# Linear attention and an MLP on one core: chunk-wise attention in eight units, another route for two heads' x, four sums on another engine, and an order made anew

## The chip, the core and the metric

The kernel runs on 1 core of one Trainium2 chip. The metric is device microseconds of one launch, less is better. The engines are named TensorE (PE; its weight loads are PEld), VectorE (DVE), ScalarE (ACT), GpSimd (POOL) and SyncE (SP, whose queue issues the DMAs).

## The reference, cut to what matters

```python
mag = np.sqrt(a_re * a_re + a_im * a_im)
scale = np.minimum(mag, 0.999) / (mag + 1e-06)
a_re_n, a_im_n = (a_re * scale, a_im * scale)
for t in range(S):                       # B, H, S, D = 4, 8, 768, 48
    ar, ai = (a_re_n[:, :, t, :, None], a_im_n[:, :, t, :, None])
    new_re = ar * S_re - ai * S_im
    new_im = ar * S_im + ai * S_re
    kv = np.einsum('bhd,bhe->bhde', k[:, :, t], v[:, :, t])
    S_re, S_im = (new_re + kv, new_im)
    y[:, :, t] = np.einsum('bhd,bhde->bhe', q[:, :, t], S_re)
x = y.transpose(0, 2, 1, 3).reshape(B * S, H * D)        # 3072 x 384
h = x @ w_in                                             # 384 x 2048
out = (0.5 * h * (1.0 + erf(h / sqrt(2)))) @ w_out       # 2048 x 384
```

Inputs are float32 for the attention; the two weights come as 64-bit words that the kernel cuts into a high and a low part.

## The kernel before, in words

**Lanes.** The recurrence is cut in time into four groups (`GROUPS`), each of two chunks: group 0 has chunks of 64 steps, group 1 too, groups 2 and 3 have chunks of 128. Within a chunk the running products of a are scanned from its middle outwards, in 128 lanes, by VectorE (`scan`: two operations a step, tiles `tt` and `bt`), and k and q are scaled by them. A group is done in slices of 8 steps, numbered s = 0 to 23 over all groups (0 to 3 are group 0, 4 to 7 group 1). Each slice needs two sums of squares, of a (`squares_a`, on tile `tab`) and of b (`squares_b`, on tile `a`), which go through ln and exp on ScalarE. `sum_of` makes such a sum on VectorE or GpSimd, or as two matmuls with the identity on TensorE (out to a bank `att`) for the first slices: a's slices 1 to `NGA` - 1 and b's 0 to `NGB` - 1. A tick of slice s handles a's slice s + 2 and b's slice s - 1; b's last slice of a group has the last of its ticks to itself. `against` writes the scaled keys and queries to DRAM (`kq<-xt`).

**Weights.** 32 pieces of the two weight matrices are loaded (`raw`), cut into high and low parts by ScalarE and VectorE (`wh`, `wi_hi`, `wo_lo`, ...), with four TensorE instructions of 384 columns a piece (`po<-wh,ident_r` twice, and one for each part with `minus`).

**Units.** 24 units are 128 tokens each of one batch entry: units 0 to 3 are steps 0 to 127 of the four entries, units 4 to 7 steps 128 to 255, and so on; so units 0 to 7 hold two chunks of 64 and units 8 to 23 one chunk of 128. A unit loads its keys and queries from DRAM (`kqn<-kq`; from unit `UT` = 8 on in pieces for VectorE's transpose), turns them (`kT`, `qT`), makes scores of 128 x 128 for four heads at a time (`att<-qT,kp`, 2 instructions a head), masks them (`kp<-att,causal`, 512 columns), and makes y: from scores and v (`att<-kp,vn`, 2 instructions a head) and from the state of the chunk's start (`att<-qT,st`). In a unit with two chunks the mask also leaves out the scores between the chunks, whose part comes through the state. Then the state is brought forward (`turn_by_pe` or `turn_state`, then `products`). y stands with heads 0 to 5 in places of 48 partitions and heads 6 and 7 apart; ScalarE and VectorE copy it out as a high and a low part, heads 0 to 5 straight to `xT`, heads 6 and 7 to `x67`, from where six copies of 16 KB put it into the free partitions of `xT`. ScalarE's copies also sum each part into a column of `flags`, from which the end of the kernel tells whether the inputs lay in its range.

**Banks.** Of PSUM's eight banks three (`own`, shown as `att`) serve sums, transposes, scores, y and states in turn (`ps_att`), two (`ph`) and three (`po`) serve the MLP. Units 0 and 1 (`early`) take banks for y and states from `ph` and two of `po`. `held` keeps a unit's later banks from falling on the one that holds its y.

**Blocks.** The MLP runs in nine blocks of 2 or 3 units. For each of 16 slices of the hidden layer nine matmuls go to `ph`, ScalarE makes gelu twice (`gh`, `gf`), VectorE or GpSimd the difference (`gl`), and nine (or six) matmuls go to `po`. A block needs the x of all its units before its first matmul.

**The order.** Nothing is issued as it is written down. Each call becomes a step of `Plan`, with its engine (or the engines between which it may choose) and a cost from a table; `order` runs a list scheduler forward and backward over all steps, with ranks that begin from the remaining path plus an offset by kind (`MORE`; `WL` weighs the lanes' VectorE chain, `BIAS` the choice among engines), keeps the best of five passes, and `issue` emits the instructions in that order on each engine. SP's queue issues the DMAs in that order too, each waiting for its input. Since all are emitted by one helper, nearly every row carries the line L427, and rows are told apart by their tiles.

Of the kernel before, what the change touches and what calls it, by code (L numbers as in the profile page):

```python
# [10 lines left out]
F32 = mybir.dt.float32  # L11
# [5 lines left out]
ALU = mybir.AluOpType  # L17
# [3 lines left out]
B, H, S, D = 4, 8, 768, 48  # L21
D2 = 2 * D
BH = B * H
C = 128
NC = S // C
NU = NC * B


GROUPS = ((0, 64), (128, 64), (256, 128), (512, 128))
# [7 lines left out]
NCC = DM // 128  # L37
# [12 lines left out]

flag_n = NSL
flag_x = flag_n + NG
flag_w = flag_x + 2 * NU
NFLAG = flag_w + 2 * NW


def dap(t, offset, dims):
    return bass.AP(t.tensor, t.offset + offset, dims)


def vap(t, dims):
    t = t[:] if not isinstance(t, bass.AP) else t
    return bass.AP(t.tensor, t.offset, [list(t.ap[0])] + dims)
# [23 lines left out]
FIRST_TABLE = TABLES[AF.Ln]  # L87
NEAR = 0.076
LOCK = True
NGA, NGB = 4, 3  # L90
UPE = 6
UT = 8
EARLIER, N_RAW, N_KP = 1, 4, 2
PASSES = 4
N_A = 4
WL = 3.892

MORE = dict(lanes0=141.86, lanes1=-1524.48, lanes2=-2225.65, lanes3=-2095.07, weights=-255.99, units=275.2, blocks=232.24)
BIAS = dict(vector=1.08, scalar=-0.75, gpsimd=1.15, sync=4.42)


class Step:
# [335 lines left out]
def lanes_and_chunks(ctx, tc, flags, a_lanes, x_lanes, v_units, w_in, w_out, out):  # L438
    nc = tc.nc
    pool = lambda name, bufs, **kw: ctx.enter_context(tc.tile_pool(name=name, bufs=bufs, **kw))  # L440
    cst = pool("cst", 1)
    dram = pool("dram", 1, space=DRAM)
    ps = pool("ps", 1, space=PSUM)
    P = Plan(nc, loose=[flags])

    def ring(name, shape, n, dtype=F32, pool=cst):
        return itertools.cycle([pool.tile(shape, dtype, name=f"{name}{i}", tag=f"{name}{i}")[:] for i in range(n)])
# [24 lines left out]
    nc.gpsimd.memset(causal, 1.0)  # L472
    nc.gpsimd.affine_select(causal, causal, pattern=[[1, 128]], compare_op=ALU.is_ge, fill=0.0, base=0, channel_multiplier=-1)

    masks = {C: causal}
    for size in (64,):
        masks[size] = cst.tile([128, 128], F32, name=f"causal{size}")
        nc.gpsimd.tensor_copy(masks[size], causal)
        for t in range(0, C - size, size):
            nc.gpsimd.memset(masks[size][t:t + size, t + size:C], 0.0)  # L480

    wi_hi = cst.tile([128, NFT, NCC, 128], F32R, name="wi_hi")
    wi_lo = cst.tile([128, NFT, NCC, 128], F32R, name="wi_lo")
# [271 lines left out]
    kps = ring("kp", [128, 4, 128], N_KP)  # L755
    xTs = ring("xT", [128, BLK, NCC, 2, 128], 2, F32R)
    x67s = ring("x67", [128, 2, 128], 1, F32R)

    def gains(g):
        p = next(ps_att)  # L760
# [25 lines left out]
    def unit(u):  # L786
# [48 lines left out]
        def bank():  # L835

            p = next(ps_early if early else ps_att)
            return bank() if any(p is x for x in held) else p
# [56 lines left out]
            else:  # L895
                P.vector.tensor_tensor(out=sf, in0=p, in1=sf, op=ALU.add)

        qT, kT, kp, pm = [], [], [], []

        def turn(hh):  # L900
            if by_dve:
# [20 lines left out]
        def scores(hh):  # L922
            p = next(ps_att)
            with P.together():
                for j in range(4):
                    P.tensor.matmul(out=p[:, j * 128:(j + 1) * 128], lhsT=kT[hh][:, j, :], rhs=qT[hh][:, j, :], start=True, stop=True)
            t = kp[hh]
            P.vector.tensor_tensor(out=t, in0=p.rearrange("p (j l) -> p j l", j=4), in1=vap(masks[chunks[0][4]], [[0, 4], [1, 128]]), op=ALU.mult)
            pm.append(t)

        def y(hh):
            with P.together():
                for h in range(hh * 4, hh * 4 + 4):
                    P.tensor.matmul(out=py[h % 2 * 64:h % 2 * 64 + 64, h // 2], lhsT=vn[:, h], rhs=pm[hh][:, h % 4], start=h < 2,
                                    stop=h > 5 and not with_state)
# [8 lines left out]
        if early:  # L947
            turned = {}
            for c0, c1 in zip(chunks[::2], chunks[1::2]):
                add_state(c0, None)  # L950
                turned[c1] = turn_by_pe(c1[0], c1[5])
            held.append(bank())
            py = held[0].rearrange("p (c l) -> p c l", c=4)
            for hh in range(2):
                turn(hh)
                scores(hh)
                y(hh)
                for c in with_state:
                    y_state(c, hh)
            for c in with_state:  # L960
                add_state(c, turned[c])
        else:
            for hh in range(2):
                turn(hh)
                scores(hh)
            held.append(bank())
            py = held[0].rearrange("p (c l) -> p c l", c=4)
            for c in chunks:
                turned = p = None
                if c[0]:  # L970
                    turned = (turn_by_pe if u < UPE else turn_state)(c[0], c[5])
                with P.together():
                    if c is chunks[0]:
                        y(0)
                        y(1)
                    if c[0]:
                        y_state(c, 0)
                        y_state(c, 1)
                    if c[0] < NP - 1:
                        p = products(c, turned)  # L980
                if p is not None:
                    add_state(c, turned, p)
# [2 lines left out]
            xblk[j] = next(xTs)  # L985
        xt, x67 = xblk[j][:, u - first_unit[j]], next(x67s)
        fc = flag_x + 2 * u
        parts = ((py[:, 3], x67[:, 0], x67[:, 1], fc), (py[:, 0:3], xt[:, :, 0], xt[:, :, 1], fc + 1))
        for at, hi, _, f in parts:
            P.scalar.activation(hi, at, AF.Copy, accum_out=flags[:, f:f + 1])  # L990
        for at, hi, lo, _ in parts:
            P.vector.tensor_tensor(out=lo, in0=at, in1=hi.bitcast(F32), op=ALU.subtract)

        for c in range(NCC):
            for p0 in (0, 64):
                P.sync.dma_start(out=xt[p0 + D:p0 + 64, c].bitcast(F32), in_=x67[p0 + c * 16:p0 + c * 16 + 16].bitcast(F32))


    ghs, gls = ring("gh", [128, BLK * C], EARLIER + 1, F32R), ring("gl", [128, BLK * C], EARLIER + 1, F32R)
# [313 lines left out]
```

## Time and profile before

| | us |
|---|---|
| median of 3 runs | 677.06 (673.62 to 678.73) |
| profiled execution, its own time | 673.5 |
| its span, first to last instruction | 671.6 |
| TensorE busy | 617.7 (92%) |
| VectorE busy | 486.4 (72%) |
| ScalarE busy | 442.6 (66%) |
| GpSimd busy | 55.1 (8%) |
| mean granted TensorE clock | 0.964 of full speed |

The profiled execution's own time goes beside the span; the 1.9 us between them lie around it. A share of the whole span is a mean over stages: lanes and weights alone at first, then units and blocks together with the rest of the lanes, then blocks with the last units. The granted clock has two levels, 0.5 (1.2 GHz) and 1.0 (2.4 GHz); a mean between them is a stretch that has both.

### The profile page before, as it was taken

To read this page: it belongs to the slowest core of one execution; us is meant where nothing else is said; L and a number is where in the kernel's file an instruction comes from. 1 tells how busy PE (TensorE), PEld (TensorE's weight loads), DVE (VectorE), ACT (ScalarE), POOL (GpSimd) and SP (SyncE) were. 2 spreads that over 40 slices of the span, in tenths; PEclk is the share of its full clock that TensorE was granted. 3 is DMA by queue.
4 is the path that set the end of the run, shared out by engine and by line. 5 is a ranking of instruction groups with operands and counts; after the bars stand their busy time and mean duration, and the time that the engine had idled before them with its cause. 6 is when DMAs were issued, how large, how long until landed. Compare 5 with 4: busy or idle time off the path is not lost.

```text
span 671.6 us, 13581 instructions
## 1 busy us (share of the span) xinstructions
PE 617.7 (92%) x4882; PEld 568.5 (85%) x4882; DVE 486.4 (72%) x1171; ACT 442.6 (66%) x1104; POOL 55.1 (8%) x95
## 2 busy tenths in 40 slices
PE   4455799988999999999999999999999999999995
PEld 2222477878789989999999998999999999999995
DVE  6999889999999999989959999945552431332121
ACT  8977789998889888787476888653343432233332
POOL 1002103012001100211000001210100000000000
PEclk9877599999999999999999999999999999999998
DMA  9268935758277565788597988697762413010000
GB/s 315 95 150 226 321 120 180 216 154 221 64 207 183 136 138 134 192 146 153 108 153 189 175 223 181 166 157 138 154 121 42 76 57 51 1 47 2 24 1 26
DMA packets 209160, 91.38 MB, mean 136 GB/s; under 512 B 168512, under 2 KB 201408, under 8 KB 209088
## 3 DMA queue, kind: packets, MB, share of 16 engines
q1 hardware_dynamic: 209088, 90.47, 56.6%
q8 instruction: 39, 0.64, 0.4%
q14 instruction: 33, 0.27, 0.1%
HBM read 61.54 MB, written 23.59 MB: 127 GB/s over the span
## 4 chain that ended last, share of the span: by engine, by line
PE 51%; DMA 2%; DVE 2%; ACT 1%; issue 1%; DVEq 0%; SPq 0%
PE po L427 21%; PE ph L427 20%; PE att L427 10%; DMA xt<-in_x_lanes_dram 1%; DMA a<-in_a_lanes_dram 0%; ACT gh L427 0%; DVE tt L427 0%; ACT st L427 0%; DVE bt L427 0%; ACT tab L427 0%; ACT L427 0%; DVE kp L427 0%; DVE gl L427 0%; ACT gf L427 0%; DVE xt L427 0%
## 5 line engine op out<-in xcount | busy, mean ns | idle before, releaser
L427 PE MATMUL ph<-xT,wi_hi 128*128 128x384 f32 (+1 forms) x864 | 208.1, 323 | 1.0 <-ACT gf L427 1.0
L427 PEld LDWEIGHTS ph<-xT,wi_hi 128*128 128x128 f32 x864 | 153.8, 188 | 3.4 <-ACT gf L427 1.8
L427 ACT ACTIVATE gh<-ph 128x384 fp32r<-128x384 f32 (+1 forms) x144 | 65.4, 454 | 135.6 <-PE ph L427 134.8
L427 DVE TENSOR_TENSOR gl<-gf,gh 128x384 fp32r<-128x384 f32 (+1 forms) x133 | 68.7, 517 | 116.0 <-ACT gf L427 115.6
L427 PE MATMUL ph<-xT,wi_lo 128*128 128x384 f32 (+1 forms) x432 | 137.0, 317 | 0.0
L427 PE MATMUL po<-wo_hi,gh 128*128 128x384 f32 x384 | 133.2, 347 | 2.3 <-ACT gh L427 2.2
L427 PE MATMUL po<-wo_lo,gh 128*128 128x384 f32 x384 | 129.6, 338 | 0.0
L427 PE MATMUL po<-wo_hi,gl 128*128 128x384 f32 x384 | 92.4, 342 | 0.0
L427 PEld LDWEIGHTS ph<-xT,wi_lo 128*128 128x128 f32 x432 | 81.2, 188 | 0.0
L427 PEld LDWEIGHTS po<-wo_hi,gh 128*128 128x128 f32 x384 | 72.1, 188 | 5.5 <-ACT gh L427 4.1
L427 PEld LDWEIGHTS po<-wo_lo,gh 128*128 128x128 f32 x384 | 72.3, 188 | 0.4
L427 DVE TENSOR_TENSOR tt<-bt,a 128x192 f32<-128x192 f32 x192 | 69.2, 360 | 0.8
L427 ACT ACTIVATE gf<-ph 128x384 f32<-128x384 f32 (+1 forms) x144 | 65.1, 452 | 2.8 <-DVE gl L427 2.7
L427 PEld LDWEIGHTS po<-wo_hi,gl 128*128 128x128 f32 x384 | 66.0, 188 | 0.9 <-issue 0.2
L427 PE MATMUL po<-wh,ident_r 128*128 128x384 f32 x64 | 34.7, 631 | 24.8 <-ACT wi_lo L427 13.5
L427 PE MATMUL att<-qT,kp 96*128 96x128 f32 x384 | 49.8, 277 | 1.3 <-DVE kp L427 0.9
L427 DVE TENSOR_TENSOR bt<-tt 128x96 f32<-128x96 f32 x192 | 49.1, 256 | 0.8
L427 PEld LDWEIGHTS att<-qT,kp 96*128 96x128 f32 x384 | 47.0, 191 | 2.4 <-ACT a L427 1.7
L427 DVE TENSOR_TENSOR kp<-att,causal 128x512 f32<-128x512 f32 x48 | 32.9, 685 | 19.0 <-PE att L427 18.9
L427 PEld LDWEIGHTS po<-wh,ident_r 128*128 128x128 f32 x64 | 12.5, 230 | 32.1 <-ACT wi_lo L427 16.4
L427 POOL TENSOR_TENSOR gl<-gf,gh 128x384 fp32r<-128x384 f32 (+1 forms) x11 | 12.7, 1158 | 265.6 <-ACT gf L427 207.4
L427 ACT ACTIVATE st<-st,gg 96x48 f32<-96x48 f32 x120 | 28.6, 326 | 1.8 <-DMA m<-st 1.8
(166 smaller groups left out, 1011.6 us busy)
## 6 DMA issues: line engine op xcount, KB each, us to landing
kqn<-kq SPq DMA_DIRECT2D x96, 128.0 KB, 3.8
xt<-in_x_lanes_dram SPq DMA_DIRECT2D x24, 384.0 KB, 4.2
kq<-xt SPq DMA_DIRECT2D x48, 192.0 KB, 3.6
a<-in_a_lanes_dram SPq DMA_DIRECT2D x20, 384.0 KB, 3.5
raw<-in_w_pieces_dram SPq DMA_DIRECT2D x16, 384.0 KB, 4.7
raw<-in_moe_w_out_dram SPq DMA_DIRECT2D x16, 384.0 KB, 5.0
vn<-in_v_units_dram SPq DMA_DIRECT2D x24, 256.0 KB, 3.8
kqn<-kq SPq DMA_DIRECT2D x8, 768.0 KB, 5.8
```

The costliest lines, as they stand in the source:

```text
L427: getattr(getattr(self.nc, engine), name)(*args, **kw)
```

## The change

- Units 0 to 7: scores are made for each chunk of 64 by itself, for all eight heads into one bank, and masked in one VectorE pass of 512 columns; y is made for each chunk into a bank of its own (`y_of`), with the state's part following at once. x is copied out chunk by chunk, so there are four ScalarE and four VectorE parts where there were two of each, with columns of their own in `flags`.
- Units 8 to 23 (`UB` = 8): `x67` goes to a tile in DRAM in one copy of 128 KB, and from there to `xT` in two copies, in place of six copies within SBUF.
- `NGA` goes from 4 to 6 and `NGB` from 3 to 5: the sums of a's slices 4 and 5 and of b's slices 3 and 4 are made by TensorE.
- `WL`, `MORE` and `BIAS` have other values, so that the order of all steps is another one.

```diff
@@ -50,7 +50,7 @@
 flag_n = NSL
 flag_x = flag_n + NG
-flag_w = flag_x + 2 * NU
+flag_w = flag_x + 2 * NU + 2 * sum(size < C for _, size in GROUPS) * B
 NFLAG = flag_w + 2 * NW
@@ -87,16 +87,17 @@
 FIRST_TABLE = TABLES[AF.Ln]
 NEAR = 0.076
 LOCK = True
-NGA, NGB = 4, 3
+NGA, NGB = 6, 5
 UPE = 6
 UT = 8
+UB = 8
 EARLIER, N_RAW, N_KP = 1, 4, 2
 PASSES = 4
 N_A = 4
-WL = 3.892
-MORE = dict(lanes0=141.86, lanes1=-1524.48, lanes2=-2225.65, lanes3=-2095.07, weights=-255.99, units=275.2, blocks=232.24)
-BIAS = dict(vector=1.08, scalar=-0.75, gpsimd=1.15, sync=4.42)
+WL = 5.36
+MORE = dict(lanes0=1180.6, lanes1=-1574.6, lanes2=-4035.5, lanes3=-2920.3, weights=-1612.5, units=-107.0, blocks=-136.5)
+BIAS = dict(vector=0.0, scalar=-1.4, gpsimd=0.7, sync=-4.7)
 class Step:
@@ -472,12 +473,9 @@
     nc.gpsimd.memset(causal, 1.0)
     nc.gpsimd.affine_select(causal, causal, pattern=[[1, 128]], compare_op=ALU.is_ge, fill=0.0, base=0, channel_multiplier=-1)
-    masks = {C: causal}
-    for size in (64,):
-        masks[size] = cst.tile([128, 128], F32, name=f"causal{size}")
-        nc.gpsimd.tensor_copy(masks[size], causal)
-        for t in range(0, C - size, size):
-            nc.gpsimd.memset(masks[size][t:t + size, t + size:C], 0.0)
+    causal64 = cst.tile([128, C // 2], F32, name="causal64")
+    for p0 in (0, 64):
+        nc.gpsimd.tensor_copy(causal64[p0:p0 + 64], causal[p0:p0 + 64, p0:p0 + 64])
     wi_hi = cst.tile([128, NFT, NCC, 128], F32R, name="wi_hi")
     wi_lo = cst.tile([128, NFT, NCC, 128], F32R, name="wi_lo")
@@ -755,6 +753,7 @@
     kps = ring("kp", [128, 4, 128], N_KP)
     xTs = ring("xT", [128, BLK, NCC, 2, 128], 2, F32R)
     x67s = ring("x67", [128, 2, 128], 1, F32R)
+    x67d = itertools.cycle([dram.tile([128, 2, 128], F32, name=f"x67d{i}") for i in range(2)])
     def gains(g):
         p = next(ps_att)
@@ -895,7 +894,7 @@
             else:
                 P.vector.tensor_tensor(out=sf, in0=p, in1=sf, op=ALU.add)
-        qT, kT, kp, pm = [], [], [], []
+        qT, kT, kp, pm, pys = [], [], [], [], []
         def turn(hh):
             if by_dve:
@@ -925,11 +924,37 @@
                 for j in range(4):
                     P.tensor.matmul(out=p[:, j * 128:(j + 1) * 128], lhsT=kT[hh][:, j, :], rhs=qT[hh][:, j, :], start=True, stop=True)
             t = kp[hh]
-            P.vector.tensor_tensor(out=t, in0=p.rearrange("p (j l) -> p j l", j=4), in1=vap(masks[chunks[0][4]], [[0, 4], [1, 128]]), op=ALU.mult)
+            P.vector.tensor_tensor(out=t, in0=p.rearrange("p (j l) -> p j l", j=4), in1=vap(causal, [[0, 4], [1, 128]]), op=ALU.mult)
             pm.append(t)
+        def scores_by_chunk():
+            p = next(ps_att).rearrange("p (h l) -> p h l", h=H)
+            t = kp[0].rearrange("p j l -> p (j l)").rearrange("p (h l) -> p h l", h=H)
+            with P.together():
+                for h in range(H):
+                    for _, _, _, t0, size, _ in chunks:
+                        P.tensor.matmul(out=p[t0:t0 + size, h], lhsT=kT[h // 4][:, h % 4, t0:t0 + size], rhs=qT[h // 4][:, h % 4, t0:t0 + size], start=True, stop=True)
+            P.vector.tensor_tensor(out=t, in0=p, in1=vap(causal64, [[0, H], [1, C // 2]]), op=ALU.mult)
+            pm.append(t)
+        def y_of(chunk):
+            i, _, _, t0, size, b = chunk
+            held.append(bank())
+            py = held[-1][:, 0:4 * size].rearrange("p (c l) -> p c l", c=4)
+            with P.together():
+                for h in range(H):
+                    P.tensor.matmul(out=py[h % 2 * 64:h % 2 * 64 + 64, h // 2], lhsT=vn[t0:t0 + size, h], rhs=pm[0][t0:t0 + size, h],
+                                    start=h < 2, stop=h > 5 and not i)
+                if i:
+                    for h in range(H):
+                        P.tensor.matmul(out=py[h % 2 * 64:h % 2 * 64 + D, h // 2], lhsT=st[b][:, h], rhs=qT[h // 4][:, h % 4, t0:t0 + size],
+                                        start=False, stop=h > 5)
+            pys.append((py, t0, size))
         def y(hh):
             with P.together():
@@ -949,33 +974,37 @@
             for c0, c1 in zip(chunks[::2], chunks[1::2]):
                 add_state(c0, None)
                 turned[c1] = turn_by_pe(c1[0], c1[5])
-            held.append(bank())
-            py = held[0].rearrange("p (c l) -> p c l", c=4)
-            for hh in range(2):
-                turn(hh)
-                scores(hh)
-                y(hh)
-                for c in with_state:
-                    y_state(c, hh)
+            turn(0)
+            turn(1)
+            scores_by_chunk()
+            for c in chunks:
+                y_of(c)
             for c in with_state:
                 add_state(c, turned[c])
         else:
             for hh in range(2):
                 turn(hh)
-                scores(hh)
-            held.append(bank())
-            py = held[0].rearrange("p (c l) -> p c l", c=4)
+                if len(chunks) == 1:
+                    scores(hh)
+            if len(chunks) == 2:
+                scores_by_chunk()
+            else:
+                held.append(bank())
+                py = held[0].rearrange("p (c l) -> p c l", c=4)
+                pys.append((py, 0, C))
             for c in chunks:
                 turned = p = None
                 if c[0]:
                     turned = (turn_by_pe if u < UPE else turn_state)(c[0], c[5])
                 with P.together():
-                    if c is chunks[0]:
+                    if len(chunks) == 2:
+                        y_of(c)
+                    else:
                         y(0)
                         y(1)
-                    if c[0]:
-                        y_state(c, 0)
-                        y_state(c, 1)
+                        if c[0]:
+                            y_state(c, 0)
+                            y_state(c, 1)
                     if c[0] < NP - 1:
                         p = products(c, turned)
                 if p is not None:
@@ -985,15 +1014,25 @@
             xblk[j] = next(xTs)
         xt, x67 = xblk[j][:, u - first_unit[j]], next(x67s)
         fc = flag_x + 2 * u
-        parts = ((py[:, 3], x67[:, 0], x67[:, 1], fc), (py[:, 0:3], xt[:, :, 0], xt[:, :, 1], fc + 1))
+        parts = []
+        for py, t0, size in pys:
+            at = slice(t0, t0 + size)
+            parts += [(py[:, 3], x67[:, 0, at], x67[:, 1, at], fc), (py[:, 0:3], xt[:, :, 0, at], xt[:, :, 1, at], fc + 1)]
+            fc += 2 * NU
         for at, hi, _, f in parts:
             P.scalar.activation(hi, at, AF.Copy, accum_out=flags[:, f:f + 1])
         for at, hi, lo, _ in parts:
             P.vector.tensor_tensor(out=lo, in0=at, in1=hi.bitcast(F32), op=ALU.subtract)
-        for c in range(NCC):
+        if u >= UB:
+            x = next(x67d)
+            P.sync.dma_start(out=x[:], in_=x67.bitcast(F32))
             for p0 in (0, 64):
-                P.sync.dma_start(out=xt[p0 + D:p0 + 64, c].bitcast(F32), in_=x67[p0 + c * 16:p0 + c * 16 + 16].bitcast(F32))
+                P.sync.dma_start(out=xt[p0 + D:p0 + 64].rearrange("p c a l -> p c (a l)").bitcast(F32), in_=dap(x, p0 * 256, [[256, 16], [16 * 256, NCC], [1, 256]]))
+        else:
+            for c in range(NCC):
+                for p0 in (0, 64):
+                    P.sync.dma_start(out=xt[p0 + D:p0 + 64, c].bitcast(F32), in_=x67[p0 + c * 16:p0 + c * 16 + 16].bitcast(F32))
     ghs, gls = ring("gh", [128, BLK * C], EARLIER + 1, F32R), ring("gl", [128, BLK * C], EARLIER + 1, F32R)
```

## Rows read from the trace of the kernel before

**Rows 1.** Windows by stage: busy us of each engine (instructions), TensorE clock, DMA.

```profile
0.00:81.00 81.00, 43.49 (x90) 22.93 (x90) 71.12 (x192) 65.11 (x164) 8.38 (x33) 0.76 0.74 216
81.00:115.00 34.00, 33.40 (x373) 26.52 (x372) 31.56 (x78) 30.68 (x83) 6.17 (x4) 0.91 0.49 156
115.00:297.00 182.00, 174.84 (x1522) 160.46 (x1518) 175.09 (x451) 161.57 (x359) 20.11 (x33) 1.00 0.66 166
297.00:440.00 143.00, 141.51 (x1225) 138.16 (x1224) 128.91 (x299) 103.44 (x248) 16.07 (x17) 1.00 0.76 163
440.00:660.00 220.00, 219.93 (x1656) 216.43 (x1655) 78.69 (x152) 79.59 (x249) 4.36 (x9) 1.00 0.35 66
```

**Rows 2.** Waits of TensorE in 0 to 81 us: total, times, longest.

```profile
PE po L427 <- ACT wi_lo L427: 13.5, 7, 2.8
```

**Rows 3.** Timelines of VectorE, SP's queue and TensorE: start, length, instructions.

```profile
60.47 0.55 DVE L427 TENSOR_TENSOR a<-a 128x384 f32<-128x384 f32 x1
...
67.01 3.07 SPq L427 DMA_DIRECT2D kq<-xt  x3
...
73.85 1.49 SPq L427 DMA_DIRECT2D kqn<-kq  x2
...
81.09 1.20 PE L427 MATMUL ph<-vn,kqn 64*64 64x48 f32 x18
```

**Rows 4.** Timeline of TensorE in unit 6: start, length, instructions.

```profile
212.94 1.05 PE L427 MATMUL att<-qT,kp 96*128 96x128 f32 x8
213.75 0.60 PE L427 MATMUL ph<-xT,wi_hi 128*128 128x384 f32 x2
...
214.45 1.09 PE L427 MATMUL att<-kp,vn 128*64 128x128 f32 x16
215.38 0.62 PE L427 MATMUL att<-qT,st 96*48 96x64 f32 x16
215.93 1.14 PE L427 MATMUL att<-vn,kqn 64*64 64x48 f32 x32
216.99 0.44 PE L427 MATMUL po<-wo_hi,gh 128*128 128x384 f32 x1
```

**Rows 5.** Groups by form, TensorE, 81 to 297 us: busy us, mean ns.

```profile
L427 PE MATMUL att<-qT,kp 96*128 96x128 f32 x128 | 17.7, 281 | 1.3 <-DVE kp L427 0.9 <-ACT a L427 0.4
```

**Rows 6.** Groups by form, VectorE, 81 to 297 us.

```profile
L427 DVE TENSOR_TENSOR kp<-att,causal 128x512 f32<-128x512 f32 x16 | 10.9, 682 | 1.4 <-PE att L427 1.3
L427 DVE SCALAR_TENSOR_TENSOR wh<-raw,wh 128x384 uint32<-128x384 uint32 x15 | 8.2, 547 | 0.0
...
L427 DVE TENSOR_SCALAR raw<-wh 128x384 uint32<-128x384 uint32 x15 | 5.4, 363 | 0.7 <-ACT square L427 0.7
...
L427 DVE TENSOR_TENSOR xT<-att,xT 128x384 fp32r<-128x384 f32 x6 | 3.3, 545 | 0.0
```

**Rows 7.** Groups by form, ScalarE, 81 to 297 us.

```profile
L427 ACT ACTIVATE xT<-att 128x384 fp32r<-128x384 f32 x6 | 2.9, 485 | 0.0
...
L427 ACT ACTIVATE x<-att 128x128 fp32r<-128x128 f32 x6 | 1.7, 278 | 0.0
...
L427 ACT ACTIVATION_READ_ACCUMULATOR x<-att 128x1 f32 x6 | 1.3, 211 | 0.0
```

**Rows 8.** Timeline of TensorE, the sum of b's slice 2.

```profile
49.52 2.76 PE L427 MATMUL att<-a,ident_r 128*128 128x384 f32 x4
```

**Rows 9.** Timelines of SP's queue and TensorE around block 3's start.

```profile
329.00 3.67 SPq L427 DMA_DIRECT2D xT<-x  x6
...
334.46 0.52 PE L427 MATMUL ph<-xT,wi_hi 128*128 128x384 f32 x2
```

**Rows 10.** DMA issues by name: number, KB, median us from issue to landing.

```profile
kqn<-kq SPq DMA_DIRECT2D x96, 128.0 KB, 3.8
...
kq<-xt SPq DMA_DIRECT2D x64, 96.0 KB, 2.7
...
xT<-x SPq DMA_DIRECT2D x144, 16.0 KB, 2.3
```

## The prediction

> **What bounds the kernel now.** I read the page's busy shares first, then the stages, then the waits inside the stage that could give. On the page TensorE looks like the one bound; the stages show that this is an average over three different limits [rows 1]. Until 81 us TensorE works 43.5 of 81 us, VectorE 71.1; what TensorE waits for there is weight pieces that ScalarE and VectorE cut up (13.5 us behind one ScalarE copy alone [rows 2]). What ends the stage is another thing, the chain of group 0: VectorE's last sum of that group at 60.5 us, the write of the scanned keys issued at 67.0, their read back issued at 73.9, the first attention matmul at 81.1 [rows 3]. From 81 to 297 us three engines are nearly full at once: TensorE 33.4 + 174.8 = 208.2 of 216 us, VectorE 31.6 + 175.1 = 206.7, ScalarE 30.7 + 161.6 = 192.3 [rows 1]. From 297 us on TensorE alone binds: 141.5 of 143, then 219.9 of 220. So the time is 81 us, plus TensorE's work behind that, plus its idle time behind it (7.8 us to 297, 1.5 to 440), plus the end. An edit is worth what it takes from one of these; freeing VectorE or ScalarE behind 297 us is worth nothing.
>
> **Scores and y of units 0 to 7.** In unit 6's stretch the scores of four heads, 8 instructions, take from 212.94 to 213.75: 101 ns each; y takes 16 instructions from 214.45 to 215.38, 58 ns; the state's part with 64 columns 16 from 215.38 to 215.93, 34 ns; the products with 48 columns 32 from 215.93 to 216.99, 33 ns [rows 4]. A head's scores are 2 instructions of 128 columns now and become 2 chunks x 2 of 64 columns with 64 stationary columns; y's 2 of 128 columns become 4 of 64. Neither new shape is in the trace; the nearest row is the state's part at 34 ns. Now: 16 x 101 + 16 x 58 = 2.54 us a unit. Then: 64 x 34.4 = 2.20. That is 0.34 us less, 2.7 us in eight units. The group by form gives the 128 score instructions of all eight units 17.7 us, 2.2 us a unit [rows 5], since units 0 and 1 start at the low clock and since each group of another form pays something at its edges; by that, 0.9 us a unit and 7.5 us. At the other end, if each instruction needs 39.8 ns, nothing is saved, and at 45 ns 2.7 us are lost. I take 4.0 us off, as the units differ between the two rows, and keep +2.7 and -7.5 for the range. All of this is on the path, TensorE being at 208 of 216 us there.
>
> The trace's 33 ns for 48 columns is more than these columns need at 2.4 GHz (20 ns), so something other than streaming sets it. The Trainium skill (TensorE: Matmul & The Clock Gate, section Wait — 56ns, not 53.3ns?) puts the floor from start to start at about 25 ns, and 64 columns at 2.4 GHz plus its 2.5 ns come to 29 ns; by that estimate the unit saves 0.68 us and eight 5.5 us. The rows are higher than the page, and the sum stays with them.
>
> **The engines beside them.** The mask becomes one VectorE pass of 512 columns where there were two: 0.68 us less a unit [rows 6]. Two sets of x parts cost more: 682 ns at 512 columns and 545 at 384 leave 1.07 ns a column and 134 ns fixed, and each of the two parts that is cut in two costs one more fixed share, 2 x 0.134 = 0.27 us. So VectorE gains 0.41 us a unit, 3.3 us in eight. ScalarE pays for the same cut: 485 ns at 384 columns and 278 at 128 leave 0.174 us fixed, and each part reads its sum out in 211 ns [rows 7]; twice 0.385 is 0.77 us a unit, 6.2 us in eight. It has 216 - 192.3 = 23.7 us free in that stretch, which is its cover; without it the 6.2 us would fall on gelu, for which TensorE waits.
>
> **Four more sums on TensorE.** They are a's slices 4 and 5 and b's slices 3 and 4. VectorE's pass of one takes 0.55 us, TensorE's four instructions took 2.76 us at 49.5 us [rows 8], when the granted clock was at its lower level, 1.2 GHz, for much of the stage (mean 0.76 [rows 1]). Three of the four fall ahead of 81 us, where TensorE has 37.5 us idle, and cost no work. But b's slice 3 is the sum at 60.5 us of the chain to the first attention matmul: 2.76 in place of 0.55 puts off the start by 2.2 us, and by 0.8 us or so if the clock is up (half of 2.76). I take 1.5. The other slices free VectorE of 1.1 us ahead of 67 us; half of that, 0.5, may reach the chain. b's slice 4 comes behind 81 us and adds 1.4 us to TensorE, at the higher clock. Together 1.5 - 0.5 + 1.4 = +2.4.
>
> **x of heads 6 and 7 through DRAM, units 8 to 23.** Six copies took 3.67 us to issue at 329.0 [rows 9], 2.3 us to land [rows 10]; the block that needs them starts at 334.46 [rows 9], 1.8 us behind the last issue. Now one write to DRAM and two reads, about half of the queue's time: 16 x 1.8 = 29 us of issue less. Each hop has to land first: 2.7 us for a 96 KB write and 3.8 for a 128 KB read [rows 10], so from the first issue some 0.6 + 2.7 + 1.2 + 3.8 = 8.3 us against 3.7 + 2.3 = 6.0; 2.3 us later at most units. While the read waits for the write, what stands behind it in SP's queue (keys of later units, state halves, outputs) waits too. TensorE has the second half of the former block to do in the meantime, so I cost it at nothing; if that cover failed at each of the six blocks made of such units, it would be 6 x 2.3 = 14 us, and below nothing there is at most the 1.5 us of idle time before 440 us.
>
> The Trainium skill (DMA: Bandwidth & Descriptors, section Anatomy of one DMA — SWDGE (gpsimd) path) says that the fixed 2 us is mostly the receipt of the write and is heaviest towards HBM, which speaks against a hop more. The rows' 2.7 us agree with it; by the page the delay would be an estimated 2 us, not 2.3.
>
> **The order made anew.** Of the parameters, the lanes' weight and the offsets move weight pieces behind the lanes of group 1 and put lanes of group 0 still further ahead; where an order puts an instruction can't be read from the trace of before. It can give back at most the idle time (9.3 us behind 81) and a part of the start; it can cost as much. I take -4.0 of the idle time, somewhat under half: VectorE is relieved of 3.3 us in a stretch where it is 96% busy, and ScalarE's 6.2 us lie in its free time.
>
> **Sum.** -4.0 + 1.5 - 0.5 + 1.4 + 0 - 4.0 = -5.6 us against the profiled execution (673.5 us: the span of 671.6 and 1.9 around it): 667.9. The median of the runs is 677.06, 1.0053 times the profiled one; the forecast goes by the median: 667.9 x 1.0053 = 671.4, and I say 671.
>
> **Rivals.** First, **the start moves** (chance 0.25, 663). Ahead of the start VectorE also cuts up sixteen weight pieces, 2 x (0.547 + 0.363) = 1.8 us each [rows 6], which the chain of group 0 doesn't need. If the new order puts eight of them behind the start, this comes some 14 us sooner. Each then costs TensorE its work later: the first stage has 90 instructions in 43.5 us at a mean clock of 0.76 [rows 1], 0.48 us each, 0.37 at the full clock, four a piece, 1.5 us, less where they were at the lower level. Eight are 9 to 12 us, so the net is -2 to -5; with the rest of the idle time, some -8 in all: 673.5 - 5.6 - 8 = 659.9, scaled 663. For it speaks that TensorE is half idle until 81; against it, that 67 to 81 us are two DMA trips that no order shortens [rows 3].
>
> Second, **nothing comes of it** (0.17, 677): the narrow shapes run at 40 ns, the gain of TensorE is nil, and the start's delay eats the relief.
>
> Third, slower, **banks held for ScalarE** (0.18, 686). Three PSUM banks serve scores, transposes, y and states from unit 2 on. Now y holds one of them, then two, until ScalarE has made four passes (2 x (0.226 + 0.211) + 2 x (0.329 + 0.211) = 1.95 us, now 1.19) and VectorE four more. ScalarE is 161.6 of 182 us busy there [rows 1]. If in each of the units 2 to 7 the transposes of the next unit, or blocks behind them in TensorE's order, wait 2.5 us for it, the longer of these times and a hand-over, that is 15 us: 673.5 - 5.6 + 15 = 682.9, scaled 686.5. It decides from 5.6 / 6 = 0.9 us a unit. For it speaks that VectorE, which could take over ScalarE's other copies, is fuller still; against it, that block matmuls can stand in between, and that TensorE's idle time there, 7.8 us, has not come of banks so far.
>
> **How the numbers follow.** The forecast, about 667 to 676 with its bounds, has 0.40. A measurement of this kernel tells some 1% from no change (the three runs spread over 0.8%). Faster by over 1% (below 670.3): 0.25 of the first rival and 0.16 of the forecast, 0.41. Slower by over 1% (above 683.8): the third, most of its spread, and an order that goes wrong for some other reason, 0.19. Within: 0.40. For 8 in 10 the range reaches past the first rival, to 657, and to the near edge of the third, 684.
>
> **What would show it.** Right: score and y instructions of 64 columns at 33 to 36 ns, TensorE's busy time ahead of 297 us 3 to 5 us lower, b's slice 3 summed on TensorE some 2 us later than now relative to its scan, ScalarE's busy time up by 6 us, first attention matmul between 79 and 84 us. Wrong: a first attention matmul well ahead of 78 us (the first rival), waits of TensorE for x or y copies from 120 to 300 us (the third), waits for x's DRAM reads at block starts, or narrow instructions at 40 ns and more. An order that changes the number of weight pieces behind the start by more than four would make the sum above wrong whatever its terms.

## The result, and the profile after

The changed kernel takes 668.31 us (median of 4 runs, 666.25 to 669.32) against 676.43 (673.62 to 678.73): a ratio of 0.9875, interval 0.9844 to 0.9906, so 1.25% faster. The forecast was 671, 0.9% faster. The profiled execution took 668.66 us, its span 666.9. Ratios and their intervals, here and below, leave out executions that took over 1.5% more than the fastest of their kernel.

Windows by stage, after:

```profile
0.00:81.00 81.00, 44.50 (x90) 22.77 (x90) 70.06 (x194) 63.54 (x157) 5.86 (x33) 0.77 0.66 194
81.00:115.00 34.00, 32.58 (x474) 24.80 (x475) 32.62 (x89) 32.42 (x97) 0.00 (x0) 0.94 0.79 240
115.00:297.00 182.00, 178.70 (x1727) 163.16 (x1726) 173.90 (x463) 163.35 (x392) 20.87 (x29) 1.00 0.61 163
297.00:440.00 143.00, 141.94 (x1220) 138.48 (x1219) 128.80 (x301) 99.62 (x234) 7.88 (x7) 1.00 0.77 182
440.00:660.00 220.00, 218.52 (x1650) 214.59 (x1648) 79.04 (x154) 80.89 (x254) 3.50 (x10) 1.00 0.28 62
```

Against [rows 1], TensorE is 211.3 of 216 us busy from 81 to 297 us, where it was 208.2: not less work in a fixed stretch, but more of the whole work done by its end. In the last window but one little differs (141.9 us for 141.5); in the last the blocks end sooner (the last row of block matmuls starts at 657.8 us, 6.05 earlier than at 663.8). The end behind the blocks takes 8.9 us in this execution, 1.3 more than before, so the span is only 4.7 shorter.

The start, timelines of TensorE, SP's queue and ScalarE, after:

```profile
64.78 1.56 PE L428 MATMUL att<-a,ident_r 128*128 128x384 f32 x4 [0.66 <-ACT a L428]
...
66.43 0.58 ACT L428 ACTIVATE a<-att,by_partition 128x384 f32<-128x384 f32 x1 [0.51 <-PE att L428]
...
71.59 2.70 SPq L428 DMA_DIRECT2D kq<-xt  x3
78.86 1.01 SPq L428 DMA_DIRECT2D kqn<-kq  x2
...
83.56 2.21 PE L428 MATMUL att<-a,ident_r 128*128 128x384 f32 x4
85.70 1.14 PE L428 MATMUL ph<-vn,kqn 64*64 64x48 f32 x32
```

Each station of the chain of [rows 3] comes some 4.6 us later: keys written at 71.6 for 67.0, first attention matmul at 85.7 for 81.1. The sum of b's slice 3 is on TensorE, 1.65 us from its first matmul to ScalarE's ln behind it; the sum of b's slice 4 (83.56) stands right ahead of attention and takes 2.1 us.

A unit of two chunks, timeline of TensorE, after:

```profile
206.51 1.15 PE L428 MATMUL att<-qT,kp 96*64 96x64 f32 x32
207.59 0.44 PE L428 MATMUL po<-wo_hi,gh 128*128 128x384 f32 x1
...
208.52 0.68 PE L428 MATMUL att<-kp,vn 64*64 64x64 f32 x16
209.13 0.65 PE L428 MATMUL att<-qT,st 96*48 96x64 f32 x16
209.72 1.14 PE L428 MATMUL att<-vn,kqn 64*64 64x48 f32 x32
```

Scores of all eight heads take 1.08 us in 32 instructions, 34 ns each; in [rows 4] four heads' scores alone took 0.81 us. y of one chunk takes 0.61 us in 16 instructions, 38 ns each, so a unit's two chunks take 1.22 us where y took 0.93: what the unit saves, it saves in the scores.

The groups by form of the other engines, 81 to 297 us, after (VectorE, then ScalarE):

```profile
L428 DVE TENSOR_TENSOR kp<-att,causal 128x512 f32<-128x512 f32 x10 | 6.9, 685 | 1.9 <-PE att L428 1.3 <-ACT tab L428 0.6
...
L428 DVE TENSOR_TENSOR xT<-att,xT 128x192 fp32r<-128x192 f32 x12 | 4.2, 350 | 0.0
L428 DVE TENSOR_TENSOR x<-att,x 128x64 fp32r<-128x64 f32 x12 | 2.6, 216 | 0.0
```

```profile
L428 ACT ACTIVATE xT<-att 128x192 fp32r<-128x192 f32 x12 | 4.0, 336 | 1.3 <-PE att L428 1.3
L428 ACT ACTIVATE x<-att 128x64 fp32r<-128x64 f32 x12 | 2.8, 232 | 0.0
L428 ACT ACTIVATION_READ_ACCUMULATOR x<-att 128x1 f32 x12 | 2.6, 216 | 0.0
```

The half parts cost what [rows 6, 7] had led to expect: 350 and 216 ns on VectorE (340 and 203 by its slope), 336 and 232 on ScalarE (329 and 226).

DMA issues by name, after:

```profile
x67d<-x SPq DMA_DIRECT2D x16, 128.0 KB, 2.5
xT<-x67d SPq DMA_DIRECT2D x32, 48.0 KB, 2.1
xT<-x SPq DMA_DIRECT2D x48, 16.0 KB, 2.7
```

The two hops land in 2.5 and 2.1 us where 2.7 and 3.8 had been taken from [rows 10]. None of TensorE's waits behind 81 us is for them.

### The profile page after: what moved, and what is told of

It is laid out like the page before. It is cut to its first block, busy times and chain, and to the rows that moved or that the text cites. A ratio compares the mean times of both kernels' runs of the same rounds, so it can differ in the third digit from the quotient of the medians.

```text
span 666.9 us, 14034 instructions
## 1 busy us (share of the span) xinstructions
PE 616.2 (92%) x5154; PEld 563.8 (85%) x5154; DVE 484.4 (73%) x1196; ACT 439.8 (66%) x1131; POOL 38.1 (6%) x79
## 4 chain that ended last, share of the span: by engine, by line
PE 74%; ACT 14%; DVE 7%; DMA 2%; issue 2%; SPq 0%; ACTq 0%; DVEq 0%
PE po L428 28%; PE ph L428 28%; PE att L428 18%; ACT square L428 3%; ACT a L428 2%; ACT tab L428 2%; DVE a L428 2%; DMA raw<-in_w_pieces_dram 2%; ACT L428 1%; DVE tab L428 1%; DVE tt L428 1%; ACT L426 1%; ACT gh L428 1%; DVE bt L428 1%; DVE kp L428 1%
## 5 line engine op out<-in xcount | busy, mean ns | idle before, releaser
L428 DVE TENSOR_TENSOR gl<-gf,gh 128x384 fp32r<-128x384 f32 (+1 forms) x142 | 73.3, 516 | 122.8 <-ACT gf L428 122.3
L428 PE MATMUL po<-wh,ident_r 128*128 128x384 f32 x64 | 32.9, 600 | 21.3 <-DVE wh L428 7.0
L428 PEld LDWEIGHTS att<-qT,kp 96*64 96x64 f32 (+1 forms) x512 | 39.0, 164 | 5.2 <-DVE qT L428 2.1
L428 PE MATMUL att<-qT,kp 96*64 96x64 f32 (+1 forms) x512 | 41.0, 250 | 1.8 <-DVE qT L428 1.5
L428 DVE TENSOR_TENSOR kp<-att,causal 128x512 f32<-128x512 f32 x40 | 27.5, 688 | 9.2 <-PE att L428 7.8
L428 ACT ACTIVATE a<-tab 128x384 f32<-128x384 f32 (+1 forms) x46 | 24.5, 533 | 5.5 <-DVE tab L428 5.4
L428 DVE STREAM_TRANSPOSE kp<-kqn 96x512 f32<-96x512 f32 x32 | 21.7, 691 | 8.6 <-PE att L428 8.4
```

Of the source, the lines that this page charges most:

```text
L428: getattr(getattr(self.nc, engine), name)(*args, **kw)
```

## The experiments

Theories that they were to tell apart: TensorE's shorter scores are the gain and the order keeps it fed (mine); the new values of the order alone are the gain; the edits alone are; or a lucky order. Ratios are to the kernel before, and 0.01 is 6.8 us. In the first six kernels the order is made anew from the steps that are left, so an experiment there shows an edit and the order that came of it. The last four keep the changed kernel's order and issue one kind of step a second time, after the order was made.

**The values alone.** The kernel before with three lines of the change:

```diff
-WL = 3.892
+WL = 5.36
-MORE = dict(lanes0=141.86, ...)
+MORE = dict(lanes0=1180.6, ...)
-BIAS = dict(vector=1.08, scalar=-0.75, gpsimd=1.15, sync=4.42)
+BIAS = dict(vector=0.0, scalar=-1.4, gpsimd=0.7, sync=-4.7)
```

> The kernel before with WL, MORE and BIAS of the changed one, nothing else. My theory, that the gain is TensorE's shorter scores and a better filled stretch from 81 to 297 us: the new values are made for other steps, so 674 to 682 us, ratio 0.995 to 1.01. Rival, that the order is the gain: 666 to 670 us, ratio 0.985 to 0.99.

Ratio 1.0064 (1.0026 to 1.0102): slower. The values alone are not the gain, as I had expected.

**Chunks alone.** The changed kernel without all else:

```diff
-NGA, NGB = 6, 5
+NGA, NGB = 4, 3
-UB = 8
+UB = 24
 (WL, MORE and BIAS as before)
```

> The kernel before with attention chunk by chunk in units 0 to 7 alone; old values of WL, MORE and BIAS, four sums fewer on TensorE, x of heads 6 and 7 by six copies everywhere. My theory: TensorE is spared about 6 us from 81 to 297 us, ratio 0.988 to 0.995 if the old values suit the new steps. Rival, that the order is the gain: 0.997 to 1.005.

1.0082 (1.0036 to 1.0127): slower, against both. Its ten executions lie far apart, between 675.7 and 689.9 us, and the profiled one is near the upper end (688.6), so no row of it is used.

**All edits with the old values.**

```diff
 (WL, MORE and BIAS as before; the rest as changed)
```

> The changed kernel with the old values of WL, MORE and BIAS. My theory: the spared TensorE work remains, but the idle time of TensorE does not fall: ratio 0.990 to 0.998. Rival, that the order is the gain: 0.998 to 1.01. Rival, that the edits alone are the gain and the values are worth nothing: 0.985 to 0.99.

1.0129 (1.0057 to 1.0202): slower, against my theory and against the edits as the gain. The row of its windows shows why: from 81 to 297 us TensorE is idle for 12.7 us and the mean granted clock is 0.95.

```profile
81.00:297.00 216.00, 203.30 (x2094) 177.44 (x2094) 201.08 (x528) 187.49 (x457) 15.81 (x30) 0.95 0.59 162
```

**Whole scores.** The changed kernel with the chunks undone:

```diff
-            turn(0)
-            turn(1)
-            scores_by_chunk()
-            for c in chunks:
-                y_of(c)
+            for hh in range(2):
+                turn(hh)
+                scores(hh)
+                y(hh)
+                for c in with_state:
+                    y_state(c, hh)
 (the units behind likewise, two x parts, the mask of 128 x 128)
```

> The changed kernel with scores and y of units 0 to 7 made whole again as in the kernel before; the other edits and the new values stay. My theory: the 6 us of TensorE come back, ratio 0.995 to 1.005. Rival, that chunks are worth nothing since VectorE binds the stretch: 0.985 to 0.99.

0.9907 (0.9871 to 0.9942), only 0.3% above the changed kernel, and the two intervals overlap: my expectation failed, and the number lies at the rival's edge. The time alone does not show that the chunks gain anything. But look at the windows of that run:

```profile
81.00:297.00 216.00, 213.74 (x1933) 192.48 (x1934) 208.21 (x535) 195.50 (x457) 15.78 (x29) 0.99 0.67 175
```

TensorE is idle for 2.3 us, less than in any other kernel here; its order happened to fill the stretch better than that of the changed kernel (4.7), and with the clock it lost 3.4 us there against 6.7 (both sums are in the table below). Its profiled execution took 3.5 us more (672.14 against 668.66), its median 1.9 us more (670.25 against 668.31). With the 3.3 us that its order gained, the chunks are worth an estimated 5 to 7 us; TensorE's rows give 5.8 (below).

**Sums undone.**

```diff
-NGA, NGB = 6, 5
+NGA, NGB = 4, 3
```

> The changed kernel with NGA, NGB = 4, 3: the four sums go back to VectorE or GpSimd. My prediction had them cost 2.4 us on balance (later start, one sum behind it): then ratio 0.981 to 0.986, the first attention matmul nearer to 81 us than to 85.7. Rival, that they relieve VectorE where it binds: 0.989 to 0.997.

1.0305 (1.0237 to 1.0373): 29 us slower than the changed kernel, far outside both expectations, though the start went the way I had said (first attention matmul at 78.1 us, 7.6 earlier). Windows of 4 us and the timeline of TensorE in that run show one of the places where it went:

```profile
188.00:192.00 4.00, 3.82 (x75) 3.18 (x73) 4.00 (x14) 3.99 (x13) 0.00 (x0) 1.00 0.47 123
192.00:196.00 4.00, 0.64 (x3) 0.59 (x3) 4.00 (x14) 3.19 (x6) 0.00 (x0) 0.79 0.60 144
196.00:200.00 4.00, 3.26 (x9) 2.15 (x8) 4.00 (x12) 3.97 (x9) 0.00 (x0) 0.50 0.51 129
200.00:204.00 4.00, 4.00 (x47) 2.66 (x47) 4.00 (x11) 2.26 (x6) 0.00 (x0) 0.50 0.36 101
...
216.00:220.00 4.00, 4.00 (x44) 3.56 (x42) 3.55 (x8) 1.88 (x4) 0.00 (x0) 0.72 0.23 64
```

```profile
195.41 1.01 PE L428 MATMUL po<-wo_hi,gl 128*128 128x384 f32 x2 [3.36 <-DVE gl L428]
196.21 0.52 PE L428 MATMUL po<-wo_hi,gh 128*128 128x384 f32 x1
196.53 0.52 PE L428 MATMUL po<-wo_lo,gh 128*128 128x384 f32 x1
```

TensorE waits 3.36 us for VectorE's `gl`, and behind that wait the granted clock is at 0.5 until about 218 us; the block matmuls start 0.32 us apart there, and 0.18 at the full clock. Those 22 us at half of the full clock are an estimated 11 us lost behind a wait of 3.4. A wait of 2.7 us shortly before, for VectorE's `m`, was not followed by it: the clock stayed at 1.00 until 192 us.

**Copies within SBUF in all units.**

```diff
-UB = 8
+UB = 24
```

> The changed kernel with six copies within SBUF for x of heads 6 and 7 in all units. My prediction costs the DRAM route at nothing: ratio 0.984 to 0.991. Rival, that the queue time it spares is a gain of its own: 0.993 to 1.0.

1.0009 (0.9978 to 1.0041), just past the rival's range and far from mine. The places that the trace shows are not the rival's, though: its windows show the clock falling at about 209 us, in units that are copied the same way in both kernels, and TensorE's only waits for copies of x behind 81 us, 0.3 us at 112 and 1.0 at 189, are for such units too.

```profile
204.00:208.00 4.00, 3.27 (x50) 2.90 (x48) 3.96 (x11) 3.97 (x9) 0.00 (x0) 1.00 0.10 25
208.00:212.00 4.00, 2.88 (x22) 2.31 (x18) 4.00 (x11) 3.72 (x9) 0.00 (x0) 0.65 0.87 263
212.00:216.00 4.00, 4.00 (x62) 3.65 (x61) 0.74 (x2) 1.04 (x5) 0.00 (x0) 0.50 1.03 326
216.00:220.00 4.00, 4.00 (x16) 4.00 (x15) 3.71 (x12) 0.85 (x2) 0.00 (x0) 0.57 0.47 120
```

What the route through DRAM is worth by itself was not separated from the order.

These can be put into one table. From 81 to 297 us, in slices of 4 us, idle is the slices' length less TensorE's busy time, and clock is the sum of each length times what is missing to a granted clock of 1.

| kernel | idle us | clock us | profiled us |
|---|---|---|---|
| before | 7.8 | 3.1 | 673.5 |
| changed | 4.7 | 2.0 | 668.7 |
| values alone | 5.5 | 2.4 | 674.5 |
| old values | 12.7 | 11.7 | 684.3 |
| whole scores | 2.3 | 1.1 | 672.1 |
| sums undone | 17.7 | 20.8 | 698.4 |
| copies within SBUF | 9.2 | 6.0 | 678.3 |

Against the changed kernel, old values lose 17.7 us more in these two columns and take 15.7 more; sums undone 31.8 and 29.7; copies within SBUF 8.5 and 9.7. So in these three nearly all of the difference is TensorE idle or at the low clock from 81 to 297 us. Whole scores lose 3.3 us less there and take 3.5 more, which is TensorE's longer work. The values alone don't fit either: 3.0 us less is lost there, and yet it takes 1.0 more; TensorE did 37.6 us of work ahead of 81 us in place of 43.5, and that work came later.

**Near values**, in the changed kernel and in the kernel before:

```diff
-WL = 5.36
+WL = 5.30
```

```diff
-WL = 3.892
+WL = 3.85
```

> The changed kernel with WL = 5.30 in place of 5.36, nothing else: another order of the same steps, with no reason to be better or worse. If orders of this kind lie close together, ratio 0.984 to 0.991, and the ratios of the other experiments can be read to some 0.3%. Rival, that the order found is a lucky one: 0.993 to 1.01.

> The kernel before with WL = 3.85 in place of 3.892, nothing else. As with the one above: 0.997 to 1.005 if orders of near values lie close together, 1.005 to 1.02 if the one of before is a lucky one.

0.9871 (0.9816 to 0.9926) and 1.0005 (0.9973 to 1.0036). The order of instructions came out the same on every engine as in the changed kernel and in the one before, so these are repeats of both and tell nothing of other orders; whether the order found is a lucky one stays open on this side. As repeats they show that both times can be had again to 0.1%. In the next four experiments each difference of two ratios is uncertain by 2.4 to 3 us.

**Scores twice**, in the kept order:

```diff
-            for engine, name, args, kw in s.calls:
+            for engine, name, args, kw in s.calls * s.times:
+            P.steps[-1].times = 2
             P.vector.tensor_tensor(out=t, in0=p, in1=vap(causal64, ...
```

> The changed kernel in its own order, with each of the 256 score instructions of units 0 to 7 issued a second time (same result written over), after the order was made, so that no other instruction moves. It adds 256 x 36 to 42 ns = 9 to 11 us of TensorE work. If TensorE binds that stretch, as my theory says, all of it comes out: 677 to 679 us against 668. Rival, that VectorE or ScalarE binds it: under 4 us come out.

1.0002 (0.9976 to 1.0027): 0.0127 above the changed kernel, 8.6 us; between the medians it is 7.5. Timeline of TensorE in that run:

```profile
129.95 2.08 PE L429 MATMUL att<-qT,kp 96*64 96x64 f32 x64
131.97 0.50 PE L429 MATMUL ph<-xT,wi_hi 128*128 128x256 f32 x2
```

64 instructions take 2.02 us where 32 took 1.08, so some 7.5 us were added in eight units, less than 256 x 34 ns = 8.7. All of it comes out within the uncertainty: TensorE's work in that stretch is on the path.

**Mask twice.**

```diff
             P.vector.tensor_tensor(out=t, in0=p, in1=vap(causal64, [[0, H], [1, C // 2]]), op=ALU.mult)
+            P.steps[-1].times = 2
```

> The changed kernel in its own order, with VectorE's mask of units 0 to 7 made twice: 8 x 0.69 = 5.5 us of VectorE work, as much as the edit spares of masks. My theory: some of it comes out, as VectorE is 96% busy there and TensorE waits for it now and then: 1 to 4 us. Rival, that VectorE binds: 5 us or more. Rival, that TensorE alone binds: under 1 us.

0.9981 (0.9964 to 0.9998): 0.0106, 7.2 us for 8 x 0.69 = 5.5 added, more than I had expected. The trace of the profiled execution, the fastest of the ten, shows less: TensorE waits 3.8 us for masks, where it had waited 0.3, and its idle time up to the last block matmul is 2.9 us longer.

```profile
PE att L429 <- DVE kp L429: 3.8, 5, 1.6
```

So at least half of VectorE's work comes out; that all of it does is not shown.

**Copies of x twice.**

```diff
             P.scalar.activation(hi, at, AF.Copy, accum_out=flags[:, f:f + 1])
+            P.steps[-1].times = 2 if u < 8 else 1
```

> The changed kernel in its own order, with ScalarE's copies of x with their sums made twice in units 0 to 7: 8 x (2 x 0.44 + 2 x 0.55) = 16 us of ScalarE work, two and a half times what the edit adds there. My theory, that ScalarE's free time covers the edit's 6 us: 2 to 8 us come out. Rival, that ScalarE binds: 12 us or more.

1.0047 (1.0014 to 1.0079): 0.0172, 11.6 us for 8 x (2 x (0.22 + 0.20) + 2 x (0.33 + 0.20)) = 15.2 added: three quarters, near the rival's number; between the profiled executions it is 8.4 us. TensorE waits longer for ScalarE's `kp`, 3.7 us for 0.2:

```profile
PE att L429 <- ACT kp L429: 3.7, 4, 1.7
```

ScalarE's free time does not cover such work in a fixed order.

**One sum twice.**

```diff
+        P.steps[-1].times = 2 if (s, some) == (3, "b2") else 1
         tiles[s][some] = p
```

> The changed kernel in its own order, with the sum of b's slice 3 on TensorE made twice, at 1.6 us for one: it stands on the chain to the first attention matmul. By my theory the start of attention is put off by about 1.4 us, and the end by 1 to 1.5 us. Rival, that the start is held by something else: under 0.5 us, which the timing can hardly tell from nothing; the place of the first attention matmul in the trace tells it.

0.9928 (0.9898 to 0.9959): 0.0053, 3.6 us. Timelines of TensorE, ScalarE and TensorE in that run:

```profile
65.10 4.71 PE L429 MATMUL att<-a,ident_r 128*128 128x384 f32 x8 [0.67 <-ACT a L429]
...
69.90 0.58 ACT L429 ACTIVATE a<-att,by_partition 128x384 f32<-128x384 f32 x1 [3.66 <-PE att L429]
...
89.17 1.21 PE L429 MATMUL ph<-vn,kqn 64*64 64x48 f32 x32
```

This is more than the 1 to 1.5 us that I had expected. The granted clock was lower at that point of this run (0.50 from 64 to 68 us, where the changed kernel had 0.93), so the doubled sum took 4.8 us for 1.65, and the first attention matmul came 3.5 us later (89.17 for 85.70). In the trace the last block matmul comes 3.8 us later: a delay of the start goes through to the end nearly one for one.

## Why the prediction was right, step by step

**What bounds** held: TensorE's work behind the start of attention, its idle time, and the start itself make the time; the doubled scores and the doubled sum show the first and the last of them passing through, in full within the uncertainty. That VectorE and ScalarE are nearly full from 81 to 297 us was read rightly, but what I made of it for ScalarE was wrong: its 23.7 us of free time are no cover. The doubled copies let 0.76 of their time through by the ratios, 0.55 by the profiled executions; at that rate the edit's 6.2 us cost an estimated 3.4 to 4.7, which VectorE's relief (3.3 us at most) does not quite pay for.

**Scores and y**, forecast -4.0 (bounds +2.7 and -7.5): start to start, without the idle time between, all score groups of TensorE took 36.3 us where they had taken 42.6, and y 23.6 for 23.1, together -5.8. The term was too small by 1.8: unit 6, by which it was mostly sized, has one of the shortest rows (0.81 us for four heads, where those of the first eight units take 0.81 to 1.16). Instructions of 64 columns took 34 to 38 ns, near the 34 of the nearest row. They did not take the 29 of the estimate by the Trainium skill (TensorE: Matmul & The Clock Gate, section Wait — 56ns, not 53.3ns?).

**Four sums**, forecast +2.4: mis-sized. The start moved by 4.6 us, and the trace tells how. VectorE's scan of b's slice 3 ended 2.2 us later (61.5 for 59.3). ScalarE's square behind it stood 2.4 us in place of 0.2, since ScalarE works in the order of issue and had stood at an earlier sum. From the square to ln it took 2.5 us for 1.7, which is the longer sum, 0.9. From ln to the write of the keys it took 0.7 us less. Timelines of VectorE and ScalarE before, then after:

```profile
59.09 0.25 DVE L427 TENSOR_TENSOR bt<-tt 128x96 f32<-128x96 f32 x1
59.53 0.83 ACT L427 ACTIVATE a<-bt 128x768 f32<-128x768 f32 x1
```

```profile
61.26 0.26 DVE L428 TENSOR_TENSOR bt<-tt 128x96 f32<-128x96 f32 x1
62.21 0.58 ACT L428 ACTIVATE tab<-att,by_partition 128x384 f32<-128x384 f32 x1 [2.06 <-PE att L428]
63.90 0.83 ACT L428 ACTIVATE a<-bt 128x768 f32<-128x768 f32 x1
```

So the prediction was right about the longer sum (0.9, against its 0.8 to 2.2), and left out what the sums ahead of it do: ScalarE waits for each of them, and its waits for TensorE's sums of a before 81 us went from 2.0 to 7.4 us:

```profile
ACT tab L428 <- PE att L428: 7.4, 5, 2.1
```

Why the scan itself ended later, by the order or by such waits, was not tried apart. But TensorE did other work meanwhile, so its continuous work began only some 2.5 us later (at 83.5 in place of 81.1), with b's slice 4, which took 2.1 us where 1.4 had been forecast, since the clock was still low. Together the later start and b's slice 4 come to +4.6; how much of the start is the sums' own and how much the order's stays open.

**DRAM** at nothing: no wait of TensorE contradicts it, and no experiment isolates it. The delay was over-sized: the read lands in 2.1 us, not 3.8.

**The order**, forecast -4.0 of idle time: TensorE's idle time from its start to the last block matmul went from 9.3 to 5.3 us, -4.0. The number is right, but it was a guess at somewhat under half, and its reasons don't carry it: ScalarE's free time is no cover, and the longest wait that went was one for a load of keys, which neither VectorE's relief nor ScalarE touches (waits of TensorE before, 81 to 660 us):

```profile
PE att L427 <- DMA kqn<-kq: 2.0, 1, 2.0
```

What the prediction lacked is the second price of a wait, TensorE's clock, and with it how much a badly fitting order costs: old values, or the sums or the route through DRAM taken back under the new ones, cost 9 to 30 us, where I had said at most what the order can give. Whole scores under the new values cost only 2 to 3.5.

Put together, the blocks' last matmul came 6.05 us sooner: +2.5 for the start, -4.5 of work (-5.8 for scores and y, +2.1 for b's slice 4, the rest -0.8: fewer products at the low clock, two more pieces of weights behind the start), -4.0 of idle time: -6.0. The forecast was -5.6. That the two agree so closely is partly luck: scores and y gave 1.8 us more than forecast, the start and b's slice 4 cost 2.2 us more, and these nearly cancel.

**The signs** that the prediction named did not all come. The narrow instructions took 34 to 38 ns for 33 to 36, the sum of b's slice 3 started 2.1 us later relative to its scan, and the order moved two pieces of weights, under the four allowed. But TensorE's busy time ahead of 297 us is 255.8 us for 251.7, where 3 to 5 us less had been expected (a fixed stretch does not get emptier when later work moves up); ScalarE's is 259.3 for 257.4, where 6 more had been expected; and the first attention matmul, at 85.7 us, came later than the 79 to 84. None of the signs of being wrong came.

**Why the medians differ by more**, 8.1 us: the executions of the kernel before differ in their clock. 65 executions of it have a median of 676.1 us at a mean granted clock of 0.958, and the time falls with the clock (correlation -0.86, 5.1 us for each 0.01). The profiled one was among the better, 0.964. The changed kernel's eight executions (with the repeats) have 0.965, where a straight line through the 65 gives 672.2 for the kernel before. So by that line, an estimate, some 3.9 us of the 7.6 between these medians go with the clock, and 3.7 are the rest. The forecast scaled a profile with a better clock than the median's; that holds for a kernel whose clock stays as it was, and the changed kernel's is higher. In the repeat of the kernel before, at 0.958, the windows show where:

```profile
84.00:88.00 4.00, 4.00 (x29) 2.90 (x27) 2.38 (x7) 2.40 (x6) 0.00 (x0) 0.50 0.37 105
88.00:92.00 4.00, 4.00 (x27) 3.43 (x27) 3.04 (x10) 3.69 (x10) 0.00 (x0) 0.50 0.32 98
92.00:96.00 4.00, 4.00 (x25) 2.56 (x25) 3.21 (x8) 2.33 (x8) 1.00 (x1) 0.87 0.30 98
```

TensorE is full from 81 us on, but the clock rises only in the last of these slices; in the profiled execution of before it rose in the slice from 84 to 88 us. In both profiles of the changed order it rose between 84 and 88. Why it does so there was not tried.

**Rivals.** The start did not move forward but back. Banks held for ScalarE are not seen: no wait of TensorE behind 81 us is longer than 1.5 us, and the longest for ScalarE, 1.2, is for a piece of weights. That nothing would come of it is excluded by the interval. Whether another order of the same steps would do as well, or the one found is a lucky one, stays open.

## What to carry to other kernels

When three engines are each some 90% busy or more in a stretch, don't count the free time of one as cover: here half to all of the added work came out on every engine that was tried. Price it so, and test that by issuing the work twice in a kept order, since taking an edit back under a scheduler measures the scheduler as well. A computed order belongs to the steps for which it was found; compare versions each with an order of its own, and look first at TensorE's idle time and its clock behind each wait. And before a profile is taken as the base of a forecast, see whether its clock is that of the median run.

## What of the hardware had not been expected

A single wait of TensorE in a dense stretch could cost several times its length: behind 3.36 us of waiting the granted clock was at its lower level for some 22 us, though TensorE was 78 to 100% busy in its slices of 4 us, while a wait of 2.7 us shortly before left it at 1.00; behind two waits of 0.7 and 1.1 us around 207 to 209 us (in the kernel with copies within SBUF) it was low for some 10 us. And executions of one program differ by up to 1.4% (670.9 to 680.6 us, the kernel before) with a mean clock that differs with them (0.965 to 0.948).
